# Moving weight casts and the second batch's preparation to GpSimd, key evacuations to VectorE, fewer idle matmuls, and a new issue order with an earlier token mix

## The chip, the cores and the metric

The kernel runs on one core of one Trainium2 chip. The metric is the device time of one execution in microseconds, median of several runs. Each run has a mean granted clock of TensorE: the share of its full clock that it was allowed, 1.00 being full and 0.50 half. A run counts as slow when it is more than 1.5% above the fastest of the same kernel; ratios use fast runs alone. That label matters here: the traces show what the slow runs of the changed kernel are, and where all runs of a kernel are disturbed, the label calls them fast (below). Spans in a profile are about 1.7 us shorter than the time of the same run.

## The reference, cut to what matters

```python
# q, k, v: 8 batches, 8 heads, 576 positions, 64 per head, float32
q_d = q.reshape(B, H, Sd, 4, D).mean(axis=3)          # pooled by 4, k and v likewise
out_up = np.repeat(sm_attn(q_d, k_d, v_d), 4, axis=2) # attention of the pooled sequence
# local attention in a band |i - j| < 4
scores = np.where(np.abs(pos[:, None] - pos[None, :]) < 4, scale * q @ k.T, -1e9)
x = (out_up + softmax(scores) @ v)                    # as B x 576 x 512
theta = x @ w_theta
yr = np.einsum('ts,bsd->btd', w_tok_r, x * cos(theta))   # token mix, 576 x 576 weights
yi = np.einsum('ts,bsd->btd', w_tok_i, x * sin(theta))
u = x + yr + yi
out = u + np.maximum(u @ w_ch, 0)                     # channel mix
```

## The kernel before

The program is a set of generators, one per kind of step. A string of letters fixes the order in which steps are emitted, one order for all engines. GpSimd's timeline keeps to it: in the kernel with the engine moves alone, below, it casts two token tiles at 60.27 us although nothing is waited for there, behind a key cast (56.19) and a mask (58.07) that stand ahead of them in the string.

```python
sequences = dict(L=batches(load), C=batches(cast), A=batches(turns), S=batches(scores), N=batches(pooled_out),
                 V=batches(outputs), T=batches(transposes), H=batches(phases), Z=batches(modulate),
                 X=batches(mix), R=batches(channels), O=batches(store),
                 l=weight_loads(), c=weight_casts(), W=weight_turns(), D=warm_up())
for s in FIRST + PERIOD * PERIODS + LAST:
    next(sequences[s])
    pin()
```

L and l load inputs and weights into one pool of eight staging slots; C and c cast them to bfloat16, which frees the slot. A turns q and k (and sums v for pooling), S, N and V are the attentions, T, H and Z transpose x, form the angles, and multiply by their cosine and sine. W turns the token weights, X is the token mix, R and O are the channel mix and its store. D is a group of six matmuls whose result nobody reads; it keeps TensorE busy, 1.46 us in the timeline below.

```python
stg = ctx.enter_context(tc.tile_pool(name="stg", bufs=8))
dve, act, gp = nc.vector.tensor_copy, nc.scalar.copy, nc.gpsimd.tensor_copy
CASTS = {0: (dve, act, gp), 1: (act, gp, gp), None: (gp, gp, gp)}   # engines for q, k, v by batch

def weight_casts():
    for i in range(2):
        act(out=wth[...], in_=staged.pop(("w", f"th{i}")))
        yield
    for ri in range(2):
        for ct in range(5):
            (gp, act)[ri](out=w_tm[ri][...], in_=staged.pop(("w", f"tok{ri}{ct}"))[...])
            yield
    ...                                                             # channel weights: gp

def warm_up():
    for i in range(WARM):                                           # WARM = 10
        ps = w1(f"wu{i}")
        for _ in range(6):
            nc.tensor.matmul(out=ps, lhsT=ident, rhs=warm, start=True, stop=True)
        yield
```

In the turns of the first two batches, TensorE's result is evacuated (copied out of the PSUM tile in which this kernel has it written) by `(dve if b == 0 and n == 1 else act)`, n = 1 being the keys. In the scores, the band mask is a product on VectorE for some tiles (`DVE_BANDS = {0: 1, 1: 2}`: all of batch 0, every other of batch 1) and two selects on GpSimd for the rest (for a tile of 128x1024, a mean of 0.85 us for the product and two of 1.09 for the selects, in the profile of before).

The softmax here doesn't subtract the row's maximum and nothing guards it: scores larger than these inputs give would overflow.

## Time and profile before

| | before |
|---|---|
| time, median of the runs at first | 285.93 us (285.27 to 288.09) |
| span of the profile | 286.0 us |
| TensorE, VectorE, ScalarE, GpSimd busy | 92, 65, 69, 51% |
| first matmul of the token mix | 68.9 us |
| last token weight cast ends | 57.4 us |

The prediction shows the slices, the stretches and the chain. Two more views bear on what follows. The first cuts the profile by single microseconds around TensorE's wait for the last token weights; columns are the length, TensorE's busy time (instructions), the granted clock, the DMA's mean share and GB/s.

```profile
54.00:55.00 1.00, 1.00 (x14) 1.00 1.34 164
55.00:56.00 1.00, 0.55 (x11) 1.00 1.31 217
56.00:57.00 1.00, 0.23 (x1) 1.00 1.08 287
57.00:58.00 1.00, 0.55 (x6) 1.00 1.14 260
58.00:59.00 1.00, 1.00 (x21) 0.91 1.37 196
```

TensorE is more empty than full for three microseconds, and behind that its clock starts to drop, to 0.91 from 58 to 59 us and to 0.50 from 59 to 65. (Of its first 24.7 us this profile has no record of the clock and prints it as full; the prediction has an idle group that took 2.74 us at 21.1.) The second is TensorE's timeline near 198 us: start, length, engine, line, operation, and in brackets any idle time before it.

```profile
197.96 0.40 PE L562 MATMUL psxt<-ident,xT 128*128 128x128 bf16 x4
198.19 1.46 PE L275 MATMUL wu<-warm,ident 128*128 128x512 bf16 x6
199.49 1.03 PE L602 MATMUL psr<-wch,uT 128*128 128x512 bf16 x4
```

An idle group (wu) sits between useful ones with no gap on either side. From this line alone one can't tell whether the channel group behind it could have started sooner.

### The profile page before, as it was taken

To read this page: it belongs to the slowest core of one execution; us is meant where nothing else is said; L and a number is where in the kernel's file an instruction comes from. 1 tells how busy PE (TensorE), PEld (TensorE's weight loads), DVE (VectorE), ACT (ScalarE), POOL (GpSimd) and SP (SyncE) were. 2 spreads that over 40 slices of the span, in tenths; PEclk is the share of its full clock that TensorE was granted. 3 is DMA by queue.
4 is the path that set the end of the run, shared out by engine and by line. 5 is a ranking of instruction groups with operands and counts; after the bars stand their busy time and mean duration, and the time that the engine had idled before them with its cause. 6 is when DMAs were issued, how large, how long until landed. Compare 5 with 4: busy or idle time off the path is not lost.

```text
span 286.0 us, 7570 instructions
## 1 busy us (share of the span) xinstructions
PE 262.6 (92%) x3022; PEld 179.9 (63%) x3022; DVE 186.2 (65%) x422; ACT 196.2 (69%) x355; POOL 145.4 (51%) x170
## 2 busy tenths in 40 slices
PE   1468777799999999999999999999999999999995
PEld 1334545476676677766777667766776675776762
DVE  4956897476568665586567665866584586765542
ACT  3567998758887888777878788778756857534121
POOL 4142376365599547895389628980880811300000
PEclk9999999969999999999999999999999999999999
DMA  7999999999994498989089926994212202201213
GB/s 191 232 239 257 231 250 247 223 201 203 224 203 103 104 190 161 224 209 238 7 192 234 207 45 158 223 226 74 65 57 76 76 10 84 75 2 55 109 58 128
DMA packets 107858, 43.57 MB, mean 152 GB/s; under 512 B 97456, under 2 KB 101552, under 8 KB 107824
## 3 DMA queue, kind: packets, MB, share of 16 engines
q1 hardware_dynamic: 107824, 43.10, 67.9%
q8 instruction: 23, 0.38, 0.6%
q14 instruction: 11, 0.09, 0.1%
HBM read 33.65 MB, written 9.44 MB: 151 GB/s over the span
## 4 chain that ended last, share of the span: by engine, by line
PE 79%; DMA 8%; DVE 6%; ACT 3%; POOL 1%; issue 1%; SPq 0%; POOLq 0%
PE psu L583 25%; PE psth L541 12%; PE psr L602 10%; PE pstr L322 5%; PE psS L414 3%; PE psloc L491 3%; PE psxt L562 3%; DMA st_q<-in_q_dram 3%; PE xTps L521 3%; DMA st_k<-in_k_dram 3%; PE psx L607 2%; DMA stw_tok<-in_moe_w_tok_i_dram 2%; PE wu L275 2%; PE psr L615 2%; PE wps L262 2%; DVE kdP L312 1%
## 5 line engine op out<-in xcount | busy, mean ns | idle before, releaser
L583 PE MATMUL psu<-WT,z 128*128 128x288 bf16 x576 | 79.5, 286 | 0.0
L583 PEld LDWEIGHTS <-z 128*128 128x128 bf16 x576 | 53.4, 98 | 15.3
L435 POOL TENSOR_SCALAR_AFFINE_SELECT pm<-pm 128x1024 bf16<-128x1024 bf16 (+1 forms) x32 | 33.6, 1050 | 38.2 <-ACT pm L422 37.3
L587 DVE TENSOR_TENSOR uT<-psu,xT 128x288 bf16<-128x288 f32 x64 | 29.1, 457 | 23.4 <-PE psu L583 23.1
L627 ACT ACTIVATE rel<-psr 128x512 f32<-128x512 f32 (+1 forms) x40 | 22.2, 555 | 31.5 <-PE psr L602 20.2
L422 ACT ACTIVATE pm<-psS 128x1024 bf16<-128x1024 f32 (+1 forms) x40 | 38.5, 985 | 6.2 <-PE psS L414 5.2
L541 PE MATMUL psth<-wth,xT 128*128 128x512 bf16 (+1 forms) x192 | 42.0, 389 | 0.3 <-DVE osb L636 0.3
L636 DVE TENSOR_TENSOR osb<-rel,psx 128x512 f32<-128x512 f32 (+1 forms) x40 | 25.3, 632 | 20.8 <-ACT rel L627 14.9
L437 POOL TENSOR_SCALAR_AFFINE_SELECT pm<-pm 128x1024 bf16<-128x1024 bf16 (+1 forms) x32 | 33.6, 1051 | 2.2
L547 ACT ACTIVATE cs<-psth,pihc 128x512 bf16<-128x512 f32 x32 | 22.0, 688 | 17.2 <-PE psth L541 15.5
L602 PE MATMUL psr<-wch,uT 128*128 128x512 bf16 x128 | 32.9, 379 | 0.1
L139 POOL CAST v_w<-st_v 128x1024 bf16<-128x1024 f32 (+1 forms) x24 | 21.3, 896 | 17.7 <-DMA st_v<-in_v_dram 14.1
L522 DVE TENSOR_TENSOR xT<-xTps,xdT 128x480 bf16<-128x480 bf16 (+1 forms) x40 | 25.3, 632 | 7.5 <-PE xTps L521 7.4
L564 DVE TENSOR_TENSOR z<-psxt,cs 128x1024 bf16<-128x1024 bf16 (+1 forms) x40 | 24.6, 632 | 8.5 <-PE psxt L562 5.2
L500 DVE TENSOR_TENSOR tmp<-psloc,rl 120x512 bf16<-120x512 f32 (+1 forms) x40 | 27.6, 691 | 1.4
L133 POOL CAST k_tm<-st_k 96x1024 bf16<-96x1024 f32 x18 | 18.4, 1036 | 10.8 <-DMA st_k<-in_k_dram 8.1
L541 PEld LDWEIGHTS <-xT 128*128 128x128 bf16 (+1 forms) x192 | 14.5, 104 | 10.8 <-issue 0.7
L133 POOL CAST q_tm<-st_q 96x1024 bf16<-96x1024 f32 x18 | 18.4, 1034 | 3.9 <-DMA st_q<-in_q_dram 3.9
L325 ACT CAST kT<-pstr 128x384 bf16<-128x384 f32 x36 | 17.6, 489 | 4.0 <-PE pstr L322 3.9
L325 ACT CAST qT<-pstr 128x384 bf16<-128x384 f32 x36 | 16.6, 481 | 4.6 <-PE pstr L322 3.7
L548 ACT ACTIVATE cs<-psth 128x512 bf16<-128x512 f32 x32 | 18.9, 592 | 0.0
L491 PE MATMUL psloc<-v_w,pm 128*128 128x65 bf16 (+1 forms) x320 | 17.4, 197 | 0.3 <-DVE tmp L500 0.3
(100 smaller groups left out, 442.7 us busy)
## 6 DMA issues: line engine op xcount, KB each, us to landing
st_v<-in_v_dram SPq DMA_DIRECT2D x32, 256.0 KB, 5.0
out_dram<-osb SPq DMA_DIRECT2D x32, 256.0 KB, 2.7
st_q<-in_q_dram SPq DMA_DIRECT2D x36, 192.0 KB, 4.7
st_k<-in_k_dram SPq DMA_DIRECT2D x36, 192.0 KB, 5.0
st_q<-in_q_dram SPq DMA_DIRECT2D x8, 288.0 KB, 3.6
st_k<-in_k_dram SPq DMA_DIRECT2D x8, 288.0 KB
st_v<-in_v_dram SPq DMA_DIRECT2D x8, 200.0 KB
stw_tok<-in_moe_w_tok_r_dram SPq DMA_DIRECT2D x4, 288.0 KB, 4.3
```

The lines of the kernel that those rows point to most:

```text
L133: eng[i](out=dst[:, 2 * c:2 * c + 2].rearrange("p c h d -> p (c h d)"), in_=staged.pop((b, f"{'qk'[i]}{c}"))[0:TR])
L325: nc.scalar.copy(out=To[:, :, TR * c:TR * c + TR], in_=ps[:, :, 0:TR])
L422: nc.scalar.activation(out=pv, in_=ps[0:kw].rearrange("p e (j w) -> p (e j) w", w=P)[:, :, 0:qn], func=AF.Exp, scale=SCL,)
L435: nc.gpsimd.affine_select(out=pv, in_=pv, compare_op=ALU.is_ge, fill=0.0, base=off, pattern=[[0, 8], [-1, qn]], channel_multiplier=1)
L437: nc.gpsimd.affine_select(out=pv, in_=pv, compare_op=ALU.is_ge, fill=0.0, base=6 - off, pattern=[[0, 8], [1, qn]], channel_multiplier=-1)
L491: nc.tensor.matmul(out=pv[0:qn, par, j, :], lhsT=pms[b][c][0:kw, 4 * par + j, 0:qn], rhs=v_w[0:kw, c, 2 * j + par, 0:65], start=(j == 0), ...
L500: nc.vector.tensor_tensor(out=tmp[0:cnt].rearrange("p (j e d) -> p e j d", e=2, j=4), in0=pv[0:cnt, :, :, 0:D], in1=rl[0:cnt].unsqueeze(3) ...
L522: nc.vector.tensor_tensor(out=xT[:, :, QS[c]:QS[c] + cnt].rearrange("p e (m j) -> p e m j", j=4), in0=ps[:, :, 0:cnt].rearrange("p e (m j) ...
L541: nc.tensor.matmul(out=th[lo:lo + n, :], lhsT=xT[:, dc, P * c:P * c + n], rhs=wth[:, dc, :], start=(dc == 0), stop=(dc == 3),)
L583: nc.tensor.matmul(out=ps[:, 0:288], lhsT=z[:, j, P * dc:P * dc + P], rhs=WT[:, j, cols], start=(j == 0), stop=(j == 8),)
L587: nc.vector.tensor_tensor(out=uT[:, dc, cols], in0=ps[:, 0:288], in1=xT[:, dc, cols], op=ALU.add)
L602: nc.tensor.matmul(out=psr, lhsT=uT[:, dc, P * c:P * c + P], rhs=wch[:, dc, :], start=(dc == 0), stop=(dc == 3),)
```

## The change

The intent: keep ScalarE free in the loading stage, have GpSimd do the casts that wait for loads, load and turn the token weights ahead of the third batch so that the mix begins sooner, and drop half of the idle matmuls. The diff, with lines of changed indentation left out and the strings cut to their first line:

```diff
-    CASTS = {0: (dve, act, gp), 1: (act, gp, gp), None: (gp, gp, gp)}
+    CASTS = {0: (dve, act, gp), None: (gp, gp, gp)}
@@ weight_casts
-            act(out=wth[...], in_=staged.pop(("w", f"th{i}")))
+            gp(out=wth[...], in_=staged.pop(("w", f"th{i}")))
-                (gp, act)[ri](out=w_tm[ri][...], in_=staged.pop(("w", f"tok{ri}{ct}"))[...])
+                gp(out=w_tm[ri][...], in_=staged.pop(("w", f"tok{ri}{ct}"))[...])
@@
-    WARM = 10
+    WARM = 5
@@ turns of batches 0 and 1
-            (dve if b == 0 and n == 1 else act)(
+            (dve if n == 1 else act)(
@@
-    DVE_BANDS = {0: 1, 1: 2}
+    DVE_BANDS = {0: 1}
@@
     FIRST = (
-        "LCLLCLACALCLCAALACLCLLALLlCALASCCSSCASSDVCNlLcLVCCNcLACCLlDLLLLcCAAAANLClllCSLADAClClASTClScLcSVTSlS"
+        "LCLACLLCAALCCLALLCALCACLAASCLDSCLSCSLAlDVSLNNLcVVCLlNClcATDALTSClCADTCSlVccLlllCcLcCCHlVLTcclHTCLcLA"
         ...                                  # 289 letters before, 232 after
     PERIOD = (...)                           # 79 letters in both
     LAST = (...)                             # 153 letters with five D before, 205 with none after
```

More of the change, by code (lines that the diff above doesn't have):

```diff
@@ L243, in weight_casts @@
         for i in range(2):
-            act(out=wth[:, 2 * i:2 * i + 2, :].rearrange("p c e -> p (c e)"), in_=staged.pop(("w", f"th{i}")))
+            gp(out=wth[:, 2 * i:2 * i + 2, :].rearrange("p c e -> p (c e)"), in_=staged.pop(("w", f"th{i}")))
             yield
@@ L247, in weight_casts @@
             for ct in range(5):
-                (gp, act)[ri](out=w_tm[ri][0:OC[ct], ct, :], in_=staged.pop(("w", f"tok{ri}{ct}"))[0:OC[ct], 0:S])
+                gp(out=w_tm[ri][0:OC[ct], ct, :], in_=staged.pop(("w", f"tok{ri}{ct}"))[0:OC[ct], 0:S])
                 yield
@@ L309, in wide_turn @@
                     nc.vector.tensor_reduce(out=qdT[:, hh, :], in_=To[:, hh, :].rearrange("p (m j) -> p m j", j=4),
-                                            axis=AX.X, op=ALU.add)
+                           axis=AX.X, op=ALU.add)
                 else:
                     nc.vector.tensor_reduce(out=kdP[:, hh, 0:4, 0:30],
-                                            in_=To[:, hh, 0:480].rearrange("p (g m j) -> p g m j", g=4, j=4),
-                                            axis=AX.X, op=ALU.add)
+                       in_=To[:, hh, 0:480].rearrange("p (g m j) -> p g m j", g=4, j=4),
+                           axis=AX.X, op=ALU.add)
                     nc.vector.tensor_reduce(out=kdP[:, hh, 4, 0:24], in_=To[:, hh, 480:576].rearrange("p (m j) -> p m j", j=4),
-                                            axis=AX.X, op=ALU.add)
+                           axis=AX.X, op=ALU.add)
         def turn(n, c):
@@ L648 @@
     FIRST = (
-        "LCLLCLACALCLCAALACLCLLALLlCALASCCSSCASSDVCNlLcLVCCNcLACCLlDLLLLcCAAAANLClllCSLADAClClASTClScLcSVTSlS"
-        "LCTAVHVLCTcHZHTZlcClNLcZlcAHVAZANLcLWACSDcNALDcLCTSCWWAAVAWWAWLCWACTWSLLHVWZVHAcClALVXLTSXCLSTXACZSS"
-        "TACCXcLSXLLACASXCSAHCNLXVZHVXCCAAHZANZROAVANHTZALTVAAXTHTCHAVCRSLSOXTXZLHLLZLNHNXLACCHCCA"
+        "LCLACLLCAALCCLALLCALCACLAASCLDSCLSCSLAlDVSLNNLcVVCLlNClcATDALTSClCADTCSlVccLlllCcLcCCHlVLTcclHTCLcLA"
+        "ZlcZClLAHAAHHLLDCSAccAWLCZSLSWCCWWSWWCCLWSCLWWSZZLNASAAlXLVClXAXLAVAAXcANAXNTVAXcATLXSCVTAHCVXTHLTZH"
+        "CRHOCZLCHLZSZZRROCOSXARLCLLROLLO"
     )
     PERIOD = (
-        "SCXZZZSXROLACCASLXAROASXRALOVANLRAVOLAXLSVCCAATXSTVACRTLSOTVCHXXHCLTHZNLACHZHNA"
+        "SSXAXAANCAXAASCNAXACNLVLAXCLAVVALAXTSSCTTRROCOVACHLVXTHTZHZHHZROCSZLLZRCLLOSRXO"
     )
@@ L657 @@
     LAST = (
-        "AXSZDRZSOZCSXAALRSXOXCNACRVAOVDSATAVXVAXARORAOSXXTASRTOSSROXSTVHXHVXTXNRZHOVHZNRRHOOSZZDSNZTROROTVXX"
-        "HVTVXXTHXTXZZHZHXZROHRZOXROXXROXROXXXXRROOXRORORODRDO"
+        "LASLNAAXAACSXCALANAACCVXCAXSSCNXVAAXCAVAAROSSTTRSOCSXTAALVRSROTSVHONLTHVLZNHZLHZHZZACVCASNXXTAVAXAAC"
+        "LCVXAVARCTSSOXATSSTXTHNXVHZZHNVHHNZSXZRZORSSOXTTVRROVHOXXXTROVXTXZTHHZHXXZZHZRORROXOXXRXOXXXROROXROR"
+        "ROORO"
     )
```

## The prediction

> **What bounds the kernel now.** I read the page's engine totals and slices first, then a cut into seven stretches, then the chain of waits from 45 to 72 us, then the timelines of TensorE, ScalarE, GpSimd and the DMA queue over the first 75 us and of TensorE over the last 90.
>
> First the page: busy time in tenths of 40 slices (7.15 us each), the granted clock, and the DMA.
>
> ```profile
> PE   1468777799999999999999999999999999999995
> PEclk9999999969999999999999999999999999999999
> ```
> ```profile
> GB/s 191 232 239 257 231 250 247 223 201 203 224 203 103 104 190 161 224 209 238 7 192 234 207 45 158 223 226 74 65 57 76 76 10 84 75 2 55 109 58 128
> ```
>
> The reader is to see two regimes. In the first eight slices (57 us) TensorE has gaps while the DMA moves 191 to 257 GB/s without a pause. Afterwards TensorE is full and the DMA has slack. One slice, the ninth, has a lowered clock. The stretches, with TensorE's busy time first after the length:
>
> ```profile
> 0.00:50.20 50.20, 31.86 (x378) 20.37 (x379) 37.13 (x101) 35.46 (x52) 22.56 (x42) 1.00 1.09 235
> 50.20:57.45 7.25, 5.47 (x59) 3.11 (x58) 3.42 (x10) 5.22 (x9) 2.52 (x3) 1.00 1.20 225
> 57.45:68.92 11.47, 11.47 (x133) 8.05 (x134) 7.96 (x19) 7.17 (x17) 7.78 (x8) 0.70 1.07 201
> 68.92:129.50 60.58, 60.22 (x756) 42.73 (x755) 40.73 (x90) 49.83 (x99) 44.62 (x48) 1.00 0.86 180
> 129.50:188.40 58.90, 58.90 (x730) 41.53 (x729) 39.68 (x89) 46.76 (x93) 40.23 (x43) 1.00 0.76 164
> 188.40:281.60 93.20, 93.20 (x972) 63.64 (x970) 56.85 (x116) 51.41 (x90) 27.70 (x29) 1.00 0.25 74
> ```
>
> 68.92 us is where the first token mix (psu, letter X of the order) starts. From there to 281.6 us TensorE lacks only 0.36 us. Of the 23.4 us that it is idle in the whole span (286.0 - 262.6), 18.3 lie before 50.2 us, 1.8 between 50.2 and 57.45, and 3.0 in the final store. So the end is, to a very good approximation, "the moment of the first mix plus all TensorE work behind it plus the last store". What sets the first mix is in the chain:
>
> ```profile
> 49.15 6.61 DMA stw_tok<-in_moe_w_tok_i_dram
> 55.76 0.02 issue
> 55.78 0.67 ACT wtm L248
> 56.45 0.38 ACT qT L325
> 56.83 0.58 ACT wtm L248
> 57.41 0.04 issue
> 57.45 0.66 PE wps L262 x6
> ```
>
> The last two token-weight tiles land at 55.8 and 56.7 us, ScalarE casts them, and only then can TensorE turn them (wps) and mix. While it waited, its clock fell: a cut by single microseconds shows it busy 0.55, 0.23 and 0.55 us between 55 and 58, then a clock of 0.50 from 59 to 65. About 6.8 us at half speed is a loss of 3.4 us.
>
> [...] six idle matmuls of 512 columns take 2.74 us at 21.1 us and 1.46 us at 27.3, and the dip above follows a poorly filled window. [...] token weights of 128x576 take a median 665 ns on GpSimd and 672 on ScalarE, q and k of 96x768 take 822 and 830. [...] mix work needs no new input per batch, so it should begin while loads still pace the rest.
>
> **The change part by part.**
>
> *Engines.* ScalarE loses four q casts of batch 1 (4 x 0.83), two theta casts (2 x 1.05), five token casts (3.4 in all) and four key evacuations (4 x 0.63): 11.3 us, all before about 57 us, where it is busy some 41 of 57. VectorE gains the evacuations at 0.74 each (3.0) and loses masks of batch 1 (two at 0.85, one at 0.55: 2.2): nearly even. GpSimd gains 3.3 + 2.1 + 3.7 of casts and three masks, each two selects of 1.09 (for the short one 0.88): 6.1; together 15.2 us. It was busy 22.6 of 50.2 us, mostly waiting for loads. Counted along the new order, between about 22 and 48 us GpSimd has some 18.5 us of casts, 70% of the time, and the new masks come only after the token casts. So I give no direct gain or loss to the engine moves: the loads pace this stage. What they buy is that a landed tile is no longer cast behind ScalarE's other work, worth perhaps 0.5 us at the last token tile.
>
> *Order of the loads.* This is the main term. Summing the sizes of the loads in the order strings, the last token tile is byte 11.92 MiB of the input before and 10.42 MiB after; the new order moves the second and third batch's loads behind it. In the trace, the load that ends at 10.47 MiB before is the second q tile of batch 2; GpSimd waits for it and starts its cast at 48.4 us. With the DMA as full as before (235 GB/s to 50 us), the last token tile then lands at about 48.4 instead of 56.7, and its cast on GpSimd ends by about 49.7.
>
> *From there to the first mix.* I price each letter by start-to-start times of TensorE in the steady part: one mix group 1.105 us, a theta group 0.865 (0.98 for the last), a channel group 1.09 (0.68), an attention score tile 0.33, an output tile 0.25 (0.35), a transposition group 0.22, a turn 0.215 to 0.26, an idle group 1.29, a weight turn 0.70. Work before the first weight turn is then 22.4 before and 22.6 after, so the waiting before it costs the same up to about 50 us. From the first weight turn to the first mix lie 10.2 us of work in the new order (15.8 in the old). The prices leave out small gaps: from 68.92 to 281.57 us the old order has 206.8 us of priced work, so the factor is 212.65 / 206.8 = 1.028. Hence the first mix at 50.0 + 10.2 x 1.028 = 60.5 us if the clock stays full.
>
> *From the first mix to the end.* In the new order 207.0 us of priced work follow the first mix, against 206.8 in the old (leaving out its last idle group, which runs beside the store): less attention work was done ahead, but five idle groups, 6.5 us, are gone from the last part. Their effect is already in these sums and isn't counted again. 207.0 x 1.028 = 212.8. The store after the last channel group took 286.0 - 281.57 = 4.4; without the idle group ahead of the last channel group some of it might overlap better, but the store also waited 1.07 us for an earlier store's buffer, so I take 4.2.
>
> *Sum.* 60.5 + 212.8 + 4.2 = 277.5 us with a warm clock throughout. I add 3.4 us x 0.55 = 1.9 for a cold phase like the one before, and 1.5 for gaps that a newly arranged order brings. Total: 281.0 us, 1.7% below 285.93.
>
> **The rivals.**
>
> *A. The cold phase stays or moves (0.55).* For it: TensorE still has to wait for the loads with hardly more work in hand, and only one idle group stands directly ahead of the weight turns (D4; the other four come much earlier). In the trace the weight turns themselves, full time, did not lift the clock for 6.8 us. Against it: at the old stall three input waits followed one another, and the new one should be shorter. Cold gives 277.5 + 3.4 + 1.5 = 282.4 us; warm gives 279.0.
>
> *B. The loads don't get faster at all.* Each staging slot of the eight is released by a cast, and now nearly all casts stand in one queue, in strict order, behind whatever GpSimd does. If a landed tile waits there, the next load is issued late and the DMA runs below 235 GB/s. For it: the DMA queue's waits name staging releases up to 4.3 us. Against it: bandwidth didn't drop in those very stretches, since several loads are still under way. It would give back 2 to 4 us: 283 to 285.
>
> *C. A new bound after the first mix.* The new order runs one batch less ahead, so data arrive at TensorE with less slack, masks of the second batch (10.5 us of GpSimd) and the third batch's casts (6.2) crowd into 50 to 67 us, and the five theta groups come in a cluster, where ScalarE needs 1.28 us per group against TensorE's 0.87. Against it: per batch of 29.47 us ScalarE is busy about 23.4 and GpSimd about 20, so both can catch up. If each of three periods lost 1 us: 283 to 284.
>
> *D. The idle matmuls in the last part were free.* If TensorE would have waited there anyway, taking them out gives nothing and up to 3.9 us of the gain becomes idle time. TensorE shows no gap around the groups at 198.2, 209.1 and 239.5 us, so the trace can't tell filled waits from delays. This would give 283 to 285.
>
> **Range and chances.** The warm case without losses ends at 277.5, the cold one with one more rival at about 285; the runs before spread by 1% (285.27 to 288.09). I predict 281.0 us, and 276.8 to 286.0 for 8 in 10. Faster by over 2% means below about 280.3, close to the middle: chance 0.43. Within 2%: 0.53. Slower by over 2%, above 291.6, needs a broken steady part: 0.04.
>
> **What would show it.** Right: the first psu matmul at 60 to 64 us; the last token cast (wtm, now on GpSimd) at 48 to 51 us; the DMA still at 225 to 250 GB/s up to there; 212 to 215 us from the first psu to the last psr; successive periods of 29.3 to 29.8 us. A clock near 0.5 for some 7 us around 50 to 60 us is rival A. GpSimd waiting little and the token tiles landing after 51 us is B; TensorE below 9 tenths after 65 us, released by ScalarE or GpSimd, is C; idle time in the last 90 us of 3 us or more is D. The prediction is wrong at its root if the first mix comes at 66 us or later, or if it comes early and the end doesn't move with it.

## The result, and the profile after

| | before | after |
|---|---|---|
| time, median | 285.6 us (285.22 to 288.09, 4 runs) | 274.45 us (273.88 to 280.63, 4 runs) |
| span of the profile | 286.0 | 272.3 |
| last token weight cast ends | 57.4 | 48.8 |
| first matmul of the token mix | 68.9 | 55.3 |
| first mix to the last full channel group (its last tile, psx) | 210.6 | 210.6 |
| from there to the end | 6.5 | 6.4 |

The ratio is 0.9572 (0.9498 to 0.9646). A ratio here is the mean time of one kernel's fast runs over that of the other's fast runs of the same rounds, so not quite the ratio of the medians quoted. One of the four runs took 280.63 us at a mean clock of 0.966; the other three had 0.986 to 0.993.

The page of the changed kernel, the same lines as before:

```profile
PE   0486988999999999999999999999999999999991
PEclk9999599999999999999999999999999999999999
GB/s 199 247 237 287 258 218 216 211 202 262 144 193 235 197 206 132 175 204 204 130 115 226 209 166 56 197 211 130 138 217 30 19 2 79 79 22 39 87 89 135
```

TensorE is full from the eighth slice on (a slice is 6.8 us). The dip of the clock is now at 27 to 34 us (a mean of 0.57), while TensorE waits for loads anyway, and none follows. Cut at the first weight turn, the first mix and the last full channel group (columns: length, then busy time of TensorE, its weight loads, VectorE, ScalarE and GpSimd, clock, DMA share, GB/s):

```profile
0.00:46.70 46.70, 31.62 (x320) 19.04 (x324) 35.85 (x95) 24.72 (x35) 24.54 (x45) 0.93 1.05 239
46.70:55.30 8.60, 8.40 (x142) 6.01 (x139) 6.74 (x16) 5.77 (x9) 7.69 (x10) 1.00 1.25 207
55.30:265.90 210.60, 209.24 (x2499) 150.09 (x2518) 144.41 (x312) 151.80 (x294) 126.99 (x133) 1.00 0.63 141
265.90:272.30 6.40, 0.87 (x16) 0.60 (x13) 1.35 (x3) 0.98 (x2) 0.00 (x0) 0.98 0.41 143
```

And the kernel before, cut at the same two late points:

```profile
68.90:279.50 210.60, 210.24 (x2435) 146.81 (x2433) 136.36 (x292) 147.41 (x279) 112.54 (x118) 1.00 0.56 128
279.50:286.00 6.50, 3.54 (x28) 1.58 (x24) 1.33 (x3) 0.97 (x2) 0.00 (x0) 1.00 0.40 141
```

The reader is to see the two equal lengths. From the first mix on, both kernels take 210.6 us and then 6.4 or 6.5. Of the 13.7 us by which the spans differ, 13.6 are won before the first mix. The chain of waits of the changed kernel, where the earlier one had ScalarE's casts:

```profile
41.09 6.39 DMA stw_tok<-in_moe_w_tok_i_dram
47.49 0.05 issue
47.54 1.29 POOL wtm L248 x2
48.83 0.04 issue
48.87 1.12 PE wps L262 x11
```

The last token tiles still gate the start, 8.6 us sooner, cast by GpSimd. From the end of the cast to the first mix it is 6.5 us instead of 11.5.

### The profile page after: what moved, and what is told of

It reads as the page before. It is cut to its first block, busy times and chain, and to the rows that moved or that the text cites. A ratio compares the mean times of both kernels' runs of the same rounds, so it can differ in the third digit from the quotient of the medians.

```text
span 272.3 us, 7503 instructions
## 1 busy us (share of the span) xinstructions
PE 250.1 (92%) x2965; PEld 175.7 (65%) x2992; DVE 188.4 (69%) x423; ACT 183.3 (67%) x338; POOL 159.2 (58%) x187
## 4 chain that ended last, share of the span: by engine, by line
PE 78%; DMA 11%; POOL 3%; DVE 2%; ACT 2%; issue 1%; SPq 0%; DVEq 0%; POOLq 0%
PE psu L583 26%; PE psth L541 11%; PE psr L602 10%; PE pstr L322 6%; DMA st_v<-in_v_dram 5%; PE psxt L562 4%; PE psS L414 4%; PE psloc L491 4%; DMA stw_th<-in_moe_w_theta_dram 4%; PE xTps L521 3%; PE psx L607 2%; DMA stw_tok<-in_moe_w_tok_i_dram 2%; PE psnd L453 2%; PE psr L615 1%; PE wps L262 1%
## 5 line engine op out<-in xcount | busy, mean ns | idle before, releaser
L435 POOL TENSOR_SCALAR_AFFINE_SELECT pm<-pm 128x1024 bf16<-128x1024 bf16 (+1 forms) x35 | 36.7, 1050 | 38.5 <-ACT pm L422 38.4
L541 PE MATMUL psth<-wth,xT 128*128 128x512 bf16 (+1 forms) x181 | 39.9, 381 | 0.8
L437 POOL TENSOR_SCALAR_AFFINE_SELECT pm<-pm 128x1024 bf16<-128x1024 bf16 (+1 forms) x35 | 36.8, 1051 | 2.4
L636 DVE TENSOR_TENSOR osb<-rel,psx 128x512 f32<-128x512 f32 (+1 forms) x40 | 25.2, 632 | 18.7 <-ACT rel L627 13.7
L602 PE MATMUL psr<-wch,uT 128*128 128x512 bf16 x114 | 32.2, 380 | 0.7
```

The source lines that it names most:

```text
L435: nc.gpsimd.affine_select(out=pv, in_=pv, compare_op=ALU.is_ge, fill=0.0, base=off, pattern=[[0, 8], [-1, qn]], channel_multiplier=1)
L437: nc.gpsimd.affine_select(out=pv, in_=pv, compare_op=ALU.is_ge, fill=0.0, base=6 - off, pattern=[[0, 8], [1, qn]], channel_multiplier=-1)
L541: nc.tensor.matmul(out=th[lo:lo + n, :], lhsT=xT[:, dc, P * c:P * c + n], rhs=wth[:, dc, :], start=(dc == 0), stop=(dc == 3),)
L602: nc.tensor.matmul(out=psr, lhsT=uT[:, dc, P * c:P * c + P], rhs=wch[:, dc, :], start=(dc == 0), stop=(dc == 3),)
L636: nc.vector.tensor_tensor(out=osb[:, 0:w], in0=rel[:, 0:w], in1=psx[:, 0:w], op=ALU.add)
```

## The experiments

In all there were 18 experiments, 17 new kernels and one repeat; each result was correct. "After" stands for the changed kernel. Times of different chips differ: the kernel before had medians of 284.5 to 286.5 us in the groups below.

### Are idle matmuls in the last part delays or fillers?

*Before, without its five late idle groups.* Edit:

```diff
-    WARM = 10
+    WARM = 5
     LAST = (  # the five D taken out
```

> The kernel before, with its five late idle groups (five of ten) taken out and nothing else changed. Theory 1 (they were plain delays: TensorE had other work ready each time): the first mix stays at 69 us, and the end comes 3.9 to 5.2 us sooner (four groups of 1.29 us lie ahead of the last channel group), a ratio of 0.982 to 0.986 to before. Theory 2 (they filled waits that come back as gaps): ratio 0.998 to 1.002, and TensorE shows about 4 us of gaps after 190 us.

Measured: 282.57 us median (281.38 to 284.88), ratio 0.9898. *After, with five late idle groups:*

```diff
-    WARM = 5
+    WARM = 10
     LAST = (  # a D ahead of two mix groups, a score tile and the last channel group, and one behind it
```

> The changed kernel with five idle groups put into its last part, at places like those of before (behind the fifth batch's modulations, in its mix, before a late score tile, ahead of the last channel group, and behind it). Theory 1 (plain delays): about 4 x 1.29 = 5.2 us longer than the changed kernel, some 279.5 us. Theory 2 (they fill waits): at most 1 us longer, 274 to 275.5 us.

Measured: three fast runs of 276.68 to 277.71 us and two slow ones of 284.89 and 285.08; ratio 0.9717. The profile is of a slow run, whose low clock (0.50 from 55 to 60 us, a mean of 0.83 from 60 to 65) ends at about 61.7 us by an estimate from these two, before its first mix at 62.2. The start of a run varies, so I read the part that holds the edit: the stretch from the first mix to the last full channel group, in the profile of the first kernel and then of the second.

```profile
65.50:273.40 207.90, 206.73 (x2416) 145.30 (x2414) 136.47 (x293) 147.13 (x278) 115.35 (x121) 1.00 0.58 133
```
```profile
62.20:276.90 214.70, 214.56 (x2540) 151.80 (x2538) 144.17 (x311) 151.77 (x295) 123.38 (x130) 1.00 0.60 135
```

Against 210.6 us, three idle groups out gave 2.7 and three in cost 4.1 (the other two lie behind this stretch); three groups are 3.9 us of matmuls. So in the changed order they are plain delays, and in the old one mostly so, with 1.2 us that had filled waits. Yet both kernels take 210.6: what the changed kernel saves by dropping them, it spends on work that the old order had done ahead. The times agree in direction, less sharply: 2.9 us fewer and 3.1 more in the means of the fast runs.

### Order alone, engines alone

*Before, with the engine moves alone:* the four edits of engines in the diff above, order and WARM as before.

> The kernel before with the engine moves alone (weight casts, second batch's casts and masks on GpSimd, its key evacuations on VectorE); order and idle groups as before. Theory 1 (load order decides when the mix starts): the last token tile still lands at about 56 us, the first mix comes at 67 to 69 us, ratio 0.99 to 1.00. Theory 3 (ScalarE's queue held the start back): first mix at 64 us or earlier, ratio 0.98 or lower.

Measured: 290.33 us (289.72 to 291.28), ratio 1.0163: longer, which neither theory had. *After's order with the engines of before:* the same edits undone.

> The changed kernel's order and idle groups with the engines as before (theta, imaginary token and batch 1's q casts and key evacuations on ScalarE, three of its masks on VectorE). Theory 1: the first mix moves by no more than 1.5 us from 55.3, and the time is 274 to 276.5 us. Theory 3: the token casts on ScalarE end later by 3 us or more, the first mix comes at 58 us or later, and the time is 278 us or more.

Measured: 283.17 us in eight runs (281.19 to 284.35), ratio 0.9894. So the order alone (with its fewer idle groups) gives about 1%, the engines alone lose 1.6%, and together they give 4.3% in fast runs. My term for the engine moves, "perhaps 0.5 us", falls. What happens with the engines alone is in GpSimd's timeline:

```profile
56.19 1.04 POOL L133 CAST k_tm<-st_k 96x1024 bf16<-96x1024 f32 x1
58.07 1.09 POOL L435 TENSOR_SCALAR_AFFINE_SELECT pm<-pm 128x1024 bf16<-128x1024 bf16 x1 [0.83 <-ACT pm L422]
59.23 1.09 POOL L437 TENSOR_SCALAR_AFFINE_SELECT pm<-pm 128x1024 bf16<-128x1024 bf16 x1
60.27 1.27 POOL L248 CAST wtm<-stw_tok 128x576 bf16<-128x576 f32 x2
```

In the old order a key cast of batch 2 and a mask of batch 1 stand ahead of the last token casts. With all of them on GpSimd, the casts on which the mix waits run at 60.3 us, although the tiles are there without any wait; they end at 61.5 instead of 57.4. The queue is right for the new order only, where the masks come behind the token casts. With the new order and the old engines, the casts of the imaginary token weights stand in ScalarE's queue:

```profile
L248 POOL CAST wtm<-stw_tok x5: 660/665/1126, 30.8 to 50.0; 128x576 bf16<-128x576 f32 x4, 64x576 bf16<-64x576 f32 x1
L248 ACT CAST wtm<-stw_tok x5: 670/672/674, 45.6 to 56.7; 128x576 bf16<-128x576 f32 x4, 64x576 bf16<-64x576 f32 x1
```
```profile
L248 ACT CAST wtm<-stw_tok x5: 671/684/707, 41.5 to 52.4; 128x576 bf16<-128x576 f32 x4, 64x576 bf16<-64x576 f32 x1
```
```profile
L248 POOL CAST wtm<-stw_tok x10: 662/666/705, 31.0 to 48.2; 128x576 bf16<-128x576 f32 x8, 64x576 bf16<-64x576 f32 x2
```

These are the token casts (count, shortest/median/longest in ns, first and last start) of the kernel before, of the new order with old engines, and of after. A cast takes the same 0.67 us on either engine; what moves is when the last one starts: 56.7, 52.4, 48.2 us.

### One engine move undone at a time

Each kernel is after with one edit undone: the theta casts (`gp` to `act`), the imaginary token casts (`gp` to `(gp, act)[ri]`), the q casts of batch 1 (`1: (act, gp, gp)` put back in CASTS), or key evacuations and masks (`b == 0 and n == 1`, `DVE_BANDS = {0: 1, 1: 2}`).

> The changed kernel with only the two theta casts back on ScalarE. Undoing all engine moves cost 8.7 us, all before the first mix. Theory 4 (a queue that works in strict order stands still behind a cast whose load is late; on ScalarE it holds up evacuations that TensorE waits for, on GpSimd mostly other casts): ScalarE waits 3 us or more for the second theta tile with the query evacuation behind it, TensorE starves near 28 to 33 us, the first mix comes at 58 us or later and the time is 277 us or more. Theory 5 (what counts is ScalarE's busy time, 2.1 us here): at most 276 us.

> The changed kernel with only the five imaginary token casts back on ScalarE (3.4 us of work). Theory 4: they are the last weights to land, and on ScalarE they wait for their loads among the theta activations and score exponentials of the first batches; the last token cast ends 2 us or more after 48.8, the first mix comes at 57.5 us or later, the time is 276.5 us or more. Theory 5: about as the theta casts alone scaled by work, at most 276.5 us. If neither, 274 to 275 us.

> The changed kernel with only batch 1's four q casts back on ScalarE (3.3 us of work). Theory 4: these loads land in the order in which they are cast, so ScalarE waits little for them; 274 to 276 us. Theory 5: about 276 to 277 us.

> The changed kernel with batch 1's key evacuations back on ScalarE and three of its masks back on VectorE. No load is waited for in any of these. Theory 4: within 1 us of the changed kernel, 273.5 to 275.5 us, first mix at 55 to 56.5 us. Theory 5 (2.5 us of work on ScalarE): 276 us or more.

| undone | times, us | mean clock of each run | first mix in the profile |
|---|---|---|---|
| theta casts | 273.94, 275.40, 279.38, 280.94 | 0.988, 0.985, 0.974, 0.961 | 55.2 |
| imaginary token casts | 275.76, 277.44, 277.82, 278.67 | 0.992, 0.983, 0.983, 0.987 | 58.7 |
| q casts | 273.83, 275.78, 280.40, 280.98 | 0.990, 0.986, 0.972, 0.966 | 57.1 |
| keys and masks | 278.12, 279.26, 279.70, 281.02 | 0.983, 0.976, 0.967, 0.966 | 60.5 |

I had expected the theta casts to cost 3 us or more and keys and masks nothing. It came out the other way round, and theories 4 and 5 both fall as general rules. The theta and q rows look like the changed kernel itself, in two groups: near 274 to 276 us and near 279 to 281 us. Only the token casts cost something at a clock of 0.983 or more, some 1.5 to 4.4 us. And keys and masks, where no load is waited for, were in the upper group in nearly all runs. The key is in the clock column, and in this profile of the kernel with keys and masks undone:

```profile
45.00:46.00 1.00, 0.36 (x4) 1.00 0.84 205
46.00:47.00 1.00, 0.14 (x2) 1.00 1.18 215
47.00:48.00 1.00, 0.77 (x11) 0.88 1.33 203
48.00:55.00 7.00, 7.00 (x72) 0.50 1.07 196
55.00:62.00 7.00, 7.00 (x73) 0.54 1.23 217
```

against the same stretches of after, in its fast profile:

```profile
45.00:46.00 1.00, 0.70 (x10) 1.00 1.07 201
46.00:47.00 1.00, 0.42 (x8) 1.00 1.34 161
47.00:48.00 1.00, 1.00 (x20) 1.00 1.38 191
48.00:55.00 7.00, 6.80 (x118) 1.00 1.22 212
55.00:62.00 7.00, 7.00 (x95) 1.00 1.05 196
```

The last token cast starts at 48.2 us in both. But ahead of the weight turns, where TensorE waits for batch 1's values, one kernel is emptier, and its clock falls to a half for 13.7 us. The first mix comes 5.2 us later for it. This was the new theory 6: the loss is the clock.

### The clock, tested

*Keys and masks undone, and one idle group added inside that gap* (1.3 us more work for TensorE):

```diff
-    WARM = 5
+    WARM = 6
-        "...SAccAWLCZ..."
+        "...SAccDAWLCZ..."
```

> The changed kernel with key evacuations and masks of batch 1 put back (that alone took 279.5 us, with TensorE's clock at 0.50 from 48 to 61 us behind a gap of 1.7 us) and one idle group added ahead of the fifth step of batch 1's value sums, inside that gap. Theory 6 (the loss was the clock[...]): clock 1.00 from 45 to 65 us, first mix at 55.5 to 57.5 us, 274 to 276 us. Theory 5 (ScalarE's extra work delayed the data): first mix stays at 59 us or later, 278 us or more. This adds 1.3 us of work to TensorE, so a gain can't come from the work.

Measured: 275.24 us (274.72 to 278.63), ratio 0.9671, where without the group it was 279.48 and 0.9805. The profile has the clock at 1.00:

```profile
45.00:46.00 1.00, 0.76 (x5) 1.00 1.01 294
46.00:47.00 1.00, 0.39 (x2) 1.00 0.85 202
47.00:48.00 1.00, 0.51 (x9) 1.00 1.21 204
48.00:55.00 7.00, 6.66 (x112) 1.00 1.18 197
55.00:62.00 7.00, 7.00 (x96) 1.00 1.24 212
```

The work added can't have made it faster; the clock, full in this profile, can. (The two groups ran on different chips with four runs each, and one run of 278.63 us at a clock of 0.988 isn't explained by it.) The first mix is at 56.5 us. *After with the same idle group:*

> The changed kernel with the same one idle group added and nothing else. Theory 6: the fast runs stay at 273.9 to 275 us or lose up to 0.7, and the slow ones (280 us and more, one of four so far, and two of five with the same start) become rare or vanish. If the slow runs have another cause they stay at a quarter to a third of the runs.

Measured: 275.07 us in six runs; four of 274.49 to 275.19, two of 277.95 and 278.98 at clocks of 0.976 and 0.972. The group costs the good runs little and did not remove the bad ones. *After without any idle group* (`WARM = 0`, the five D of FIRST taken out):

> The changed kernel without any idle groups, so 6.5 us less TensorE work, all of it ahead of the weight turns. Theory 6: the clock falls in the gaps before the token tiles land (0.5 in most of 28 to 60 us), the first mix comes at 58 us or later, 277 us or more. If the loads alone set the first mix: 54.5 to 56 us, 273 to 275 us.

Measured: 279.95 us (277.60 to 283.76), with 6.5 us less work; its profile has a clock of 0.51 from 48 to 58 us and the first mix at 58.9. All four runs were above 277 us, at clocks of 0.945 to 0.976. So the early idle groups that are left pay for themselves, as far as four runs show, while the late ones did not.

*Before with two idle groups in its own gap* (two D ahead of the second weight turn, `WARM = 12`):

> The kernel before with two idle groups added where TensorE waits for the last token tiles (55 to 58 us). Theory 6: no dip of the clock at 58 to 66 us, first mix at 65.5 to 67 us instead of 68.9, ratio 0.988 to 0.995, although 2.6 us of work are added. Otherwise: ratio 1.00 to 1.01.

Measured: 288.03 us in 16 runs (285.78 to 293.97), ratio 1.0081. This is a miss. The profile does show the clock at 1.00 from 54 to 66 us, but the first mix at 68.1 us: the 2.6 us of idle work took back most of the 3.4 us. And not all runs of before have the dip that was profiled: 6.8 us at half clock make a mean of 0.988, and 11 of the 39 runs beside this one had 0.993 or more. In these cases idle matmuls in a gap were worth it where 13.7 us at half clock lay behind it, and not where 6.8 did.

*The new order with the old engines, and the one idle group:*

> The changed kernel's order with the engines of before (283.2 us; first mix at 64.5 us, clock 0.76 on average from 45 to 66 us) and the one added idle group ahead of the fifth value-sum step. It splits the 8.7 us that the engine moves are worth in the new order into clock and data. If it is the clock alone: first mix at 56 to 57.5 us, 275 to 276.5 us. If it is data alone (the last imaginary token cast on ScalarE ends at 53 instead of 48.8 us): first mix at 64 us or later, 282.5 us or more. I expect a split: no cold clock behind 50 us, first mix at 59.5 to 61.5, 278 to 280 us.

Measured: 283.36 us (280.13 to 284.30), no better than without. Its gap isn't where I put the group: TensorE was busy 0.38 and 0.42 us in the two microseconds from 55 to 57, waiting behind ScalarE's token casts, and the clock fell there (0.51 from 57 to 67 us). So it does not split clock from data. The runs of one kind do: all eight of the old engines had clocks of 0.963 to 0.973 with a median of 283.2 us, and the six runs of after at such a clock (0.961 to 0.975, this and the repeat below) have a median of 280.9. Some 2.3 us is later data, and the rest of the 8.7 us, about 6.4, is the clock. This split rests on runs of different chips, so it is an estimate.

### The load order

*After with four loads of batch 2 (1.5 MiB) put ahead of the last two token tiles,* casts likewise:

```diff
-        "...clHTCLcLA" "ZlcZClLAHAAHHLLDCSAccAWLCZSLSWCCWWSWWCC..."
+        "...clHTCLcLL" "LLLAZlcZClAHAAHHDCSACCCCccAWZSLSWWWSWWC..."
```

> The changed kernel with four loads of batch 2 (1.5 MiB) moved ahead of the last two token tiles, and their casts with them: the load order before, nearly. Theory 1: at 235 GB/s this is 6.7 us; the last token cast ends at 54 to 56 us instead of 48.8 and the first mix comes at 60 to 63 us, with a cold clock at 64 to 67; time 279 to 286 us. If the load order isn't what sets the first mix: within 1.5 us of the changed kernel.

Measured: 287.21 us in 20 runs (284.82 to 289.35), ratio 1.0061, all at clocks of 0.951 to 0.968. The last token cast starts at 56.4 us instead of 48.2, 8.2 us later where 6.7 were expected (GpSimd stood 1.54 us for TensorE ahead of the first moved cast), and the first mix comes at 67.5 because TensorE then runs at 0.50 from 48 us on. Against after's own runs at a low clock (280.9) it is 6.3 us. Load order is the largest single part of the change: undone alone, it takes the whole gain away.

### What the slow runs are, and a better version

*After with the second theta cast moved behind three casts of batch 1,* because GpSimd had stood 4.2 us for it in a slow profile:

```diff
-        "...LlNClcATDALTSClCADTCSlV..."
+        "...LlNClATDALTSClCADTCcSlV..."
```

> The changed kernel with the cast of the second theta tile moved behind three casts of batch 1 in GpSimd's queue. In the slow profile of the late-idle kernel GpSimd stood 4.2 us for that tile while landed tiles lay uncast, and loads dipped to 146 GB/s. If this standstill makes the slow runs: none above 277 us in six, first mix at 53.5 to 55.5 us, median 272.5 to 274.5 us. If not: a quarter to a third of the runs stay at 278 us or more.

Measured: 273.06, 274.01, 275.28 and 279.35, 281.27, 282.49 us. Three of six are slow: that theory falls. *After with that move, the one idle group ahead of the weight turns, and four output buffers* (`tag="osb", bufs=4`):

> The changed kernel with the theta cast moved, the one idle group added, and four output buffers in place of two (the last two sums waited 1.1 and 0.4 us for the stores of earlier ones). Expected: the stretch from the last full channel group to the end falls from 6.4 to 5.4 us, slow runs vanish, 271.5 to 274 us. If the buffers aren't the wait that sets the end, the stretch stays at 6.4.

Measured: four runs of 272.43 to 273.10, two of 280.62. The stretch at the end fell from 6.4 to 5.4 us as expected; the last sums no longer wait for a store. In after it was

```profile
267.23 0.69 DVE L636 TENSOR_TENSOR osb<-rel,psx 128x512 f32<-128x512 f32 x1 [1.08 <-DMA out_dram<-osb]
268.30 0.42 DVE L636 TENSOR_TENSOR osb<-rel,psx 128x256 f32<-128x256 f32 x1 [0.39 <-DMA out_dram<-osb]
```

*After with the gap filled by useful work:* the weight turns that need only the real token tiles, cast by 39 us, go ahead of the step that waits for value loads, with two more idle groups there and four output buffers.

```diff
-        for j in range(9):
+        for j in (0, 2, 4, 6, 1, 3, 5, 7, 8):
-        "...LLDCSAccAWLCZSLSWCCWWSWWCCLWSCLWWSZZL..."
+        "...LLDCSAWWWWDccDALCZSLSWCCWWSWWCCLSCLSZZL..."
```

> The changed kernel made robust in the gap: the four weight turns that need only the real token tiles (cast by 39 us) go ahead of the step of the value sums that waits for batch 1's value loads, with two idle groups around; four output buffers as in a_both. Theory 6: no half clock from 44 to 66 us in any run, so no run above 277 us in six; first mix at 54 to 56 us, tail 5.4 us, median 271 to 273.5 us. If slow runs have a cause beyond the gap at 44 to 48 us, a third of the runs stay at 279 us or more.

*And after once more, on the same chip:*

> The changed kernel again, unaltered, on the same chip, to count its slow runs beside those of a_best: 274 to 275 us in the fast ones, one or two of six at 278 us or more, and those with a mean clock of 0.97 or lower.

Measured: the filled version 273.77 to 275.70 us in all six runs (median 274.32, ratio 0.9592), at clocks of 0.989 to 0.998; the 271 to 273.5 us that I expected it missed. After itself 274.65 us once and 279.79 to 281.49 five times, median 280.64. The profile of such a run of after, and then of the filled version:

```profile
44.00:45.00 1.00, 0.17 (x2) 1.00 1.11 195
45.00:46.00 1.00, 0.39 (x2) 1.00 0.96 121
46.00:47.00 1.00, 0.00 (x0) 1.00 1.26 206
...
48.00:55.00 7.00, 7.00 (x80) 0.57 1.17 209
55.00:62.00 7.00, 7.00 (x68) 0.50 1.26 217
```
```profile
44.00:45.00 1.00, 1.00 (x11) 1.00 1.09 186
45.00:46.00 1.00, 1.00 (x17) 1.00 1.14 301
46.00:47.00 1.00, 1.00 (x13) 1.00 0.83 138
...
48.00:55.00 7.00, 7.00 (x98) 1.00 1.26 186
55.00:62.00 7.00, 6.75 (x101) 1.00 1.24 211
```

The two profiles of after, a fast and a slow run of one kernel, separate the clock from the data: the last token cast starts at 48.2 us in both, but in the slow one the first mix comes at 59.7 us instead of 55.3, and the clock stays at half to 62.6 us, which takes another 1.4. These 5.8 us are the whole difference of the spans. So the slow runs of the changed kernel, as far as this one profile shows, are runs in which the gap ahead of the weight turns is deeper (TensorE busy 0.56 us in the three from 44 to 47, against 2.12 in the three from 45 to 48 of the fast run) and the clock falls behind it, to 0.50 instead of 1.00. Filling it removed them in six runs of six, at a cost of about 2 us in the first mix (57.3 us) that the shorter end partly returns. The version with the best single times is the one with both small edits (272.4 to 273.1 us when fast); the one that keeps its time is the filled one. Both beat the kernel before. Against the changed kernel the filled one wins by its median on the same chip; its fast runs are no faster (ratio to before 0.9592 against 0.9572), and that of the other, 0.9552, can't be told from 0.9572 either.

## Why the prediction was wrong

The prediction was 281.0 us in 276.8 to 286.0, with 0.43 for faster by over 2%. The median was 274.45, below the range. The step that failed is the moment of the first mix: 60.5 us with a full clock, where the profile has 55.3. By its steps:

- **From the first mix to the end: right, the exactness by luck.** 212.8 + 4.2 = 217.0 us predicted; 272.3 - 55.3 = 217.0 measured. Cut where the prediction cuts, at the end of the last channel group (266.7 us), the parts are 211.4 and 5.6: two errors of 1.4 us that cancel. The pricing of letters held to that, and so did the claim that the idle groups' removal cancels against less work done ahead. Rival C (a new bound after the first mix) did not happen: TensorE lacks 1.4 of 210.6 us.
- **Loads: right, slightly late.** "The last token tile then lands at about 48.4 [...] its cast on GpSimd ends by about 49.7": it landed at 47.5 and the cast ended at 48.8. So rival B did not happen: the DMA moved 239 GB/s up to 46.7 us.
- **First weight turn: mis-sized.** I let the weight turns begin when the last token tile was cast, at 50.0 us. The first one needs only real tiles, and began at 46.7. That is 3.3 us.
- **Work up to the first mix: mis-sized.** "a weight turn 0.70" was read from the profile of before, where the turns ran at half clock. In after, three turns in a row took 1.26 us, 0.42 each, and the nine turns with the other work took 8.6 us instead of 10.2 x 1.028 = 10.5. That is 1.9 us. A price was taken from a stretch that the prediction itself names as cold.
- **Allowances: not needed in fast runs.** The 1.9 us for a cold phase and 1.5 for gaps. Together the four make 8.6 us, and 281.0 - 8.6 = 272.4, the span. (I compared a sum of spans with times that are 1.7 us longer; without this slip the miss would have been larger.)
- **Rival A: right in kind, wrong in size.** It is the state that decides between 274.5 and 280.9 us. I gave it 3.4 us, the loss seen before; it is about 6.4 by the estimate above and 5.8 between the two profiles, as the clock stayed low for 13.7 us and not 6.8. Over the ten runs of after, six were of that kind, close to the 0.55 that I gave. That the slow runs' 280.9 us lie so near 281.0 is luck: they have the early data that I foresaw and twice the cold phase. The ratio of 0.9572 leaves them out; the median of the repeat, 280.64 us, is 2.1% below the 286.53 of before beside it.
- **Engine moves: wrong.** "I give no direct gain or loss to the engine moves: the loads pace this stage." Undone together they cost 8.7 us. By the estimate above some 2.3 us of it is later data, above all the imaginary token casts, and the larger part the clock; that ScalarE's extra work is what widens the gap is argued from the profiles, not tested apart. The statement counted busy time and loads, and left out how long TensorE stands in one piece.
- **Rival D: as the prediction said, the trace could not tell.** The runs could: the late idle groups were delays of 0.9 to 1.4 us each.

How deep must the gap be? Summed over three microseconds that I chose by eye, TensorE was busy 0.56 us in after's slow run, 1.27 in keys and masks undone and 1.33 in before, where the clock fell to 0.50 behind the gap; and 1.66 (keys and masks with the idle group) and 2.12 us (after's fast run), where it stayed at 1.00. But the old engines with one idle group fell, to a mean of 0.51, after 1.80 us. So this sum sorts five of the six profiles, and the depth that decides is not shown. Nor did a full TensorE end the low clock soon. The half-clock stretches, worked out from the clock in the partly lowered microseconds at either end, lasted 6.8 us (before), 10.2 (no idle groups), 13.7 (keys and masks undone, and the slow run of after) and 17.1 (the slow run with the theta cast moved); in the last of these TensorE was busy 16.00 of 16.00 us, from 49 to 65 us, at a clock of 0.50. In the changed kernel such a fall cost an estimated 6.4 of 274.5 us, 2.3%, and came in some of its runs and not in others. What stays open is why one run is emptier than the next.

## What to carry to other kernels

Ask of a wait of TensorE how long it stands in one piece, not only how much it stands in total: here a gap of two or three microseconds, which by itself cost no more than its length, was followed by 6.8 to 17.1 us at half clock just where the critical work began, and useful work moved into it kept all six runs fast. When engine assignment and issue order both change, test each alone, because a queue that suits one order can be wrong for another (here the order alone gave -1.1%, the engines alone +1.6%, both together -4.3%). And take the price of an operation from a stretch with the clock that it will have: a weight turn took 0.70 us where the clock was 0.50 and 0.42 where it was 1.00.
